# Linear attention with elu+1 features: v loaded straight into a padded tile, relu(k) on GpSimd

## The chip, the cores and the metric

The kernel runs on one core of one Trainium2 chip. The metric is the device time of one execution in microseconds, taken as a median over runs. The engines are TensorE (PE), VectorE (DVE), ScalarE (ACT), GpSimd (POOL) and SyncE (SP); SyncE here only issues DMAs, which 16 DMA engines carry out.

## What is computed

There are 32 heads (B = 1, H = 32) of S = 2048 tokens with D = 128, all in bfloat16. Each of q, k, v and the output has 16.8 MB.

```python
phi_q = jnp.where(q > 0, q + 1, jnp.exp(q)) + 1e-6
phi_k = jnp.where(k > 0, k + 1, jnp.exp(k)) + 1e-6
kv  = jnp.einsum("bhsd,bhse->bhde", phi_k, v)
z   = jnp.einsum("bhsd->bhd", phi_k)
num = jnp.einsum("bhqd,bhde->bhqe", phi_q, kv)
den = jnp.einsum("bhqd,bhd->bhq", phi_q, z)[..., None] + 1e-6
return num / den
```

The attention is not causal: each head sums a 128x128 matrix kv over all tokens and then applies it to every query.

## The kernel before

**Layout.** A head's 2048 tokens lie on 128 partitions with 16 tokens each, so a head of q, k or v is a tile of 128 x 16 x 128 elements, 4 KB a partition. Tokens are permuted over partitions by this in the same way everywhere, and the sums don't mind.

**The feature map in two parts.** phi(x) is computed as (min(exp(x), 1) + 1e-6) + relu(x). ScalarE makes exp (`ek`, line 350; `eq`, line 386), VectorE the min and the add in place (`em`, line 353; `emq`, line 388). relu(k) is made into the tile `rk_sb`: the first 8 of the 16 tokens by VectorE (`rkd`, line 356), the last 8 by GpSimd (`rkp`, line 360). relu(q) comes from PSUM after the transpose, half by ScalarE (`rqa`, line 392) and half by VectorE (`rqb`, line 395). The two parts are never added: PE multiplies each and accumulates.

**v and its ones.** To get z with the same products, v has a column of ones beside its 128 columns. v is loaded into `v_sb`, packed; GpSimd copies it to `v1_sb` (`v1`, line 364), where a token has 136 elements (128 of v, then ones, written once at the start by `v1ones`, line 315, two memsets for the two buffers). `v1_sb` has two buffers, `v_sb` seven.

**PE** does for each head: 16 transposes of q (`T`, line 382), 32 products of 129 columns for kv and z (`kv`, line 371, two halves `kv.0` and `kv.1`: 16 tokens times the two parts), and 38 products for the output (`n`, lines 403, 408, 410, in two groups). ScalarE brings kv from PSUM to SBUF (`kvs`, line 376). VectorE takes the reciprocal of the denominators (`r`, line 417) and multiplies into the output tile (`f`, line 424), in two groups, of 12 and of 4 tokens. SyncE stores a head (`st`, line 432).

**Order.** Each engine has a list of operations, written out by hand in `ORDER`, which it executes in that order. An operation waits on semaphores for what it depends on: data, and buffers (`freed`) that must have been used up. q, k and v have 7 buffers each (`NI`), the output 12 (`NO`), exp(k) and relu(k) 2. On GpSimd there is one more rule, `gate`: from the fourth head on, the copy of v of head h waits for `r(h-3).0` and relu(k) of head h for `f(h-3).0`, which sets them beside certain VectorE instructions.

**DMAs.** SyncE issues all loads but the first of v (ScalarE) and all stores, in one list, in which the stores lie some way behind the loads: `st12` follows `ldv24`, and after the last load (`ldq31`) the stores of heads 19 to 31 are left. A load reads 32 runs of 16 KB (four partitions each) and writes 128 rows of 4 KB, each to one partition:

```python
runs = bass.AP(t.tensor, t.offset, [[RUN * NT * D, P // RUN], [1, RUN * NT * D]])
flat = bass.AP(to.tensor, to.offset, [list(to.ap[0]), [1, NT * D]])
```

Of the kernel before, what the change touches and what calls it, by code (L numbers as in the profile page):

```python
# [6 lines left out]
P = 128  # L7
# [1 line left out]
ENGINES = ("PE", "DVE", "ACT", "POOL", "SP")  # L9
NH = 32  # L10
BY_ACT = ('ldv0.0',)
NI, NO, NE, NR, NV, NQ, NK = 7, 12, 2, 2, 2, 2, 2
WARM = (15, 4, 4)
RUN = 4
QUEUE = {mybir.EngineType.SP: "qSPDynamicHW", mybir.EngineType.Activation: "qActDynamicHW"}
HALVES = ((0, 8), (8, 16))
# [3 lines left out]
def k_parts(h):  # L20
    return HALVES if h == 0 else WHOLE
# [3 lines left out]
    return WHOLE  # L25


v_parts = k_parts


def q_parts(h):
    return HALVES if h == 0 else ((0, 8), (8, 12), (12, 16)) if h == NH - 1 else WHOLE
# [3 lines left out]
    return HALVES  # L36


RKP = (8, 8, 8, 8, 8, 8, 8, 8, 8, 8, 8, 8, 8, 8, 8, 8, 8, 8, 8, 8, 8, 8, 8, 8, 8, 8, 8, 8, 8, 8, 8, 8)
NA = (8, 8, 8, 8, 8, 8, 8, 8, 8, 8, 8, 8, 8, 8, 8, 8, 8, 8, 8, 8, 8, 8, 8, 8, 8, 8, 8, 8, 8, 8, 8, 16)  # L40


def rkp_parts(h):
    return ((16 - RKP[h], 16),) if RKP[h] else ()


def rkd_parts(h):
    return tuple((a, min(b, 16 - RKP[h])) for a, b in k_parts(h) if a < 16 - RKP[h])

# [12 lines left out]
    return ((0, 6), (6, 12), (12, 16)) if h == NH - 1 else WHOLE  # L62


def gate(name, h):
    if h < 3:
        return []
    return [f"r{h - 3}.0"] if name == "v1" else [f"f{h - 3}.0"]


BANK = ((0, 8), (8, 16))
# [6 lines left out]
def rqb_parts(h):  # L78
    if na(h) == 16:
        return ()  # L80
    if h == NH - 1:
# [15 lines left out]
        n30.0 n30.1 n31.0 n31.1 n31.2  # L97
    """,
    "DVE": """
        ones eps0 rkd0.0 em0.1 em0.0 eps1 v1ones0 eps2 rkd1.0 rqb0.0 emq0.1 v1ones1 em1.0 emq0.0 rkd2.0 rqb1.0 em2.0  # L100
        emq1.0 rkd3.0 r0.0 f0.0 em3.0 rqb2.0 r0.1 rkd4.0 f0.1 r1.0 emq2.0 f1.0 em4.0 rqb3.0 r1.1 rkd5.0 f1.1 r2.0
        emq3.0 f2.0 em5.0 rqb4.0 r2.1 rkd6.0 f2.1 r3.0 emq4.0 f3.0 em6.0 rqb5.0 r3.1 rkd7.0 f3.1 r4.0 emq5.0 f4.0
        em7.0 rqb6.0 r4.1 rkd8.0 f4.1 r5.0 emq6.0 f5.0 em8.0 rqb7.0 r5.1 rkd9.0 f5.1 r6.0 emq7.0 f6.0 em9.0 rqb8.0
        r6.1 emq8.0 f6.1 r7.0 rkd10.0 f7.0 em10.0 rqb9.0 r7.1 rkd11.0 f7.1 r8.0 emq9.0 f8.0 em11.0 rqb10.0 r8.1
        rkd12.0 f8.1 r9.0 emq10.0 f9.0 em12.0 rqb11.0 r9.1 rkd13.0 f9.1 r10.0 emq11.0 f10.0 em13.0 rqb12.0 r10.1
        rkd14.0 f10.1 r11.0 emq12.0 f11.0 em14.0 rqb13.0 r11.1 rkd15.0 f11.1 r12.0 emq13.0 f12.0 em15.0 rqb14.0
        r12.1 rkd16.0 f12.1 r13.0 emq14.0 f13.0 em16.0 rqb15.0 r13.1 rkd17.0 f13.1 r14.0 emq15.0 f14.0 em17.0
        rqb16.0 r14.1 rkd18.0 f14.1 r15.0 emq16.0 f15.0 em18.0 rqb17.0 r15.1 rkd19.0 f15.1 r16.0 emq17.0 f16.0
        em19.0 rqb18.0 r16.1 f16.1 rkd20.0 r17.0 emq18.0 f17.0 em20.0 rqb19.0 r17.1 f17.1 emq19.0 r18.0 rkd21.0
        f18.0 em21.0 r18.1 rqb20.0 f18.1 rkd22.0 r19.0 emq20.0 f19.0 em22.0 r19.1 rqb21.0 f19.1 emq21.0 r20.0  # L110
        rkd23.0 f20.0 em23.0 r20.1 rqb22.0 f20.1 emq22.0 r21.0 rkd24.0 f21.0 em24.0 rqb23.0 r21.1 f21.1 emq23.0
        r22.0 rkd25.0 f22.0 em25.0 rqb24.0 r22.1 rkd26.0 f22.1 r23.0 emq24.0 f23.0 em26.0 r23.1 rqb25.0 f23.1
        emq25.0 r24.0 rkd27.0 f24.0 em27.0 r24.1 rqb26.0 f24.1 rkd28.0 r25.0 emq26.0 f25.0 em28.0 r25.1 rqb27.0
        f25.1 emq27.0 r26.0 rkd29.0 f26.0 em29.0 rqb28.0 r26.1 rkd30.0 f26.1 r27.0 emq28.0 f27.0 em30.0 r27.1
        rqb29.0 f27.1 rkd31.0 r28.0 emq29.0 f28.0 em31.0 rqb30.0 r28.1 f28.1 r29.0 emq30.0 f29.0 emq31.0 r29.1 f29.1
        emq31.1 r30.0 f30.0 r30.1 f30.1 emq31.2 r31.0 f31.0 r31.1 f31.1 r31.2 f31.2
    """,
    "ACT": """
        exp ldv0.0 ek0.1 ek0.0 eq0.1 rqa0 eq0.0 ek1.0 eq1.0 kvs0 ek2.0 rqa1 kvs1 ek3.0 eq2.0 kvs2 rqa2 ek4.0 eq3.0 kvs3 rqa3
# [6 lines left out]
        ek30.0 eq29.0 kvs29 rqa29 ek31.0 eq30.0 kvs30 rqa30 eq31.0 eq31.1 kvs31 eq31.2 rqa31  # L126
    """,
    "POOL": """
        ident0 ident rkp1.0 rkp0.0 v10.0 v10.1 v11.0 v12.0 rkp2.0 v13.0 rkp3.0 v14.0 rkp4.0 v15.0 rkp5.0 v16.0
        rkp6.0 v17.0 rkp7.0 v18.0 rkp8.0 v19.0 rkp9.0 v110.0 rkp10.0 v111.0 rkp11.0 v112.0 rkp12.0 v113.0 rkp13.0  # L130
        v114.0 rkp14.0 v115.0 rkp15.0 v116.0 rkp16.0 v117.0 rkp17.0 v118.0 rkp18.0 v119.0 rkp19.0 v120.0 rkp20.0
        v121.0 rkp21.0 v122.0 rkp22.0 v123.0 rkp23.0 v124.0 rkp24.0 v125.0 rkp25.0 v126.0 rkp26.0 v127.0 rkp27.0
        v128.0 rkp28.0 v129.0 rkp29.0 v130.0 rkp30.0 v131.0 rkp31.0
    """,
    "SP": """
        ldk0.0 ldq0.0 ldk1.0 ldq1.0 ldv1.0 ldk2.0 ldv2.0 ldq2.0 ldk3.0 ldv3.0 ldk4.0 ldq3.0 ldv4.0 ldk5.0
# [22 lines left out]
class Program:  # L159
# [10 lines left out]
    def add(self, eng, key, fn, deps=(), dma=None, inc=True):  # L170
        assert key not in self.op, key
        self.op[key] = (eng, fn, tuple(deps), dma, inc)
# [71 lines left out]
def bass_standalone__linear_attn_elu__prompt_kernel(nc: bass.Bass, q: bass.AP, k: bass.AP, v: bass.AP, out: bass.AP):  # L244
    B, H, S, D = q.shape
    assert D == P and S == 16 * P and B * H == NH
    NT = S // P
    bf16, fp32, i32 = mybir.dt.bfloat16, mybir.dt.float32, mybir.dt.int32
    NC = D + 1
    NW = D + 8  # L250
    BIG = 3.4028234663852886e38

    qf, kf, vf, of = (t.rearrange("b h s d -> (b h) s d") for t in (q, k, v, out))
    rows = lambda t, h: t[h].rearrange("(p j) d -> p j d", j=NT)

    with ExitStack() as es:
# [8 lines left out]
            return es.enter_context(nc.semaphore(f"la_s{names[0]}"))  # L265

        sb = lambda shape, dt=bf16: alloc(nc.sbuf_tensor, shape, dt)
        k_sb, q_sb, v_sb = (sb([P, NI, NT, D]) for _ in range(3))
        em_sb, rk_sb = sb([P, NE, NT, D]), sb([P, NR, NT, D])
        v1_sb = sb([P, NV, NT, NW])  # L270
        emq_sb, rq_sb = sb([P, NQ, NT, D]), sb([P, NQ, NT, D])
        kvs_sb = sb([P, NK, NW])
        rden_sb = sb([P, 2, NT], fp32)
        o_sb = sb([P, NO, NT, D])
        ident, ones, epsr = sb([P, P]), sb([P, P]), sb([P, 3])
# [4 lines left out]
        kv_ps = o_ps[:, KV0:KV0 + NC]  # L280

        pr = Program(sem)
        add = pr.add

        def over(name, h, parts, t0, t1):
            return [f"{name}{h}.{i}" for i, (a, b) in enumerate(parts(h)) if a < t1 and t0 < b]

        def every(name, h, parts):
            return [f"{name}{h}.{i}" for i in range(len(parts(h)))]

        def freed(n, h, *names):
            return [d for name, parts in names for d in every(name, h - n, parts)] if h >= n else []

        def fs(h, banks):
            return [f"f{h}.{i}" for i, (t0, nb, n, b0) in enumerate(groups(h))
                    if set(banks) & set(range(b0, b0 + nb))]
# [4 lines left out]
        def rks(h, t0=0, t1=NT):  # L301
            return over("rkd", h, rkd_parts, t0, t1) + over("rkp", h, rkp_parts, t0, t1)
# [8 lines left out]
        add("DVE", "eps2", lambda g: g.memset(epsr[32:33, :], ec), ["eps0"])  # L311
        add("DVE", "ones", lambda g: g.memset(ones[:], 1.0))
        add("ACT", "exp", lambda e: e.activation(first_sb[:, 0:1], ones[:, 0:1], ACT.Exp), ["ones"])
        for s in range(NV):
            add("DVE", f"v1ones{s}", lambda g, s=s: g.memset(v1_sb[:, s, :, D:D + 2], 1.0))

        def warm(key, n):
            def g(e):
# [13 lines left out]

        def load(name, dst, src, h, i, t0, t1, last):
            t = src[h]
            runs = bass.AP(t.tensor, t.offset, [[RUN * NT * D, P // RUN], [1, RUN * NT * D]])
            to = dst[:, h % NI]
            flat = bass.AP(to.tensor, to.offset, [list(to.ap[0]), [1, NT * D]])
            add("ACT" if f"ld{name}{h}.{i}" in BY_ACT else "SP", f"ld{name}{h}.{i}", lambda e: copy(e, flat, runs),
                last, dma=f"{name}{h % NI}.{i}")

        def head(h):
# [2 lines left out]
            for i, (a, b) in enumerate(ld_parts(h)):  # L344
                load("q", q_sb, qf, h, i, a, b, freed(NI, h, ("T", t_parts)))
            for i, (a, b) in enumerate(ld_parts(h)):
                load("v", v_sb, vf, h, i, a, b, freed(NI, h, ("v1", v_parts)))

            for i, (a, b) in enumerate(k_parts(h)):
                add("ACT", f"ek{h}.{i}", lambda e, a=a, b=b: e.activation(  # L350
# [8 lines left out]
            for i, (a, b) in enumerate(rkp_parts(h)):  # L359
                add("POOL", f"rkp{h}.{i}", lambda e, a=a, b=b: e.tensor_scalar(  # L360
                    rk_sb[:, h % NR, a:b], k_sb[:, h % NI, a:b], BIG, 0.0, op0=ALU.min, op1=ALU.max),
                    over("ldk", h, ld_parts, a, b) + freed(NR, h, ("kv", kv_parts)) + gate("rkp", h))
            for i, (a, b) in enumerate(v_parts(h)):
                add("POOL", f"v1{h}.{i}", lambda e, a=a, b=b: e.tensor_copy(  # L364
                    v1_sb[:, h % NV, a:b, 0:D].bitcast(i32), v_sb[:, h % NI, a:b].bitcast(i32)),
                    over("ldv", h, ld_parts, a, b) + freed(NV, h, ("kv", kv_parts)) + gate("v1", h))
            for i, (a, b) in enumerate(kv_parts(h)):
                def g(e, a=a, b=b):
                    for j in range(a, b):
                        for part, src in ((0, em_sb[:, h % NE]), (1, rk_sb[:, h % NR])):  # L370
                            ins = e.matmul(kv_ps, lhsT=src[:, j], rhs=v1_sb[:, h % NV, j, 0:NC],  # L371
                                           start=(j + part == 0), stop=(j == NT - 1 and part == 1))
                    return ins
                add("PE", f"kv{h}.{i}", g, over("em", h, k_parts, a, b) + rks(h, a, b) + over("v1", h, v_parts, a, b)
                    + [f"v1ones{h % NV}"] + ([f"kvs{h - 1}"] if h else []) + (fs(h - 3, [5]) if h >= 3 else []))
            add("ACT", f"kvs{h}", lambda e: e.activation(kvs_sb[:, h % NK, 0:NC], kv_ps, ACT.Copy),  # L376
                every("kv", h, kv_parts) + freed(NK, h, ("n", groups)))

# [99 lines left out]
```

## Time and profile before

| | |
|---|---|
| median of 3 runs | 171.18 us (170.42 to 171.69) |
| the profiled execution | 169.46 us, its span 168.2 us |
| granted TensorE clock | 0.996 |
| busy: PE, DVE, ACT, POOL | 158.9, 152.0, 153.6, 86.2 us |
| DMA | 67.53 MB in 9532 packets, mean 402 GB/s; the queue of the loads and stores has 96.6% of 16 engines |
| HBM | 50.33 MB read, 16.78 MB written |
| GpSimd: relu(k), copies of v | 32 x 1387 ns, 33 x 1253 ns |
| VectorE: relu(k) | 32 x 435 ns |
| issue to landing, median | k 18.8, q 19.7, v 19.2, stores 19.1 us |

How to read it: the times come from one execution under the profiler. The span runs from the first to the last instruction; the execution's time has some 1.3 us more around it. "Busy" is time in which an engine executes something. A group line gives line, engine, operation, tiles, shapes and count, then the busy time, the mean of one in ns, the engine's idle time before, and what ended that. A line of waits gives who waited for whom, the total in us, how often, and the longest. A line of a timeline gives start, duration, engine, line, operation and count. In the lines of slices each digit is the busy share of one fortieth of the span in tenths. Counts of packets go by reads: a load's 16 KB run is one packet, whatever rows it is written to.

### The profile page before, as it was taken

To read this page: it belongs to the slowest core of one execution; us is meant where nothing else is said; L and a number is where in the kernel's file an instruction comes from. 1 tells how busy PE (TensorE), PEld (TensorE's weight loads), DVE (VectorE), ACT (ScalarE), POOL (GpSimd) and SP (SyncE) were. 2 spreads that over 40 slices of the span, in tenths; PEclk is the share of its full clock that TensorE was granted. 3 is DMA by queue.
4 is the path that set the end of the run, shared out by engine and by line. 5 is a ranking of instruction groups with operands and counts; after the bars stand their busy time and mean duration, and the time that the engine had idled before them with its cause. 6 is when DMAs were issued, how large, how long until landed. Compare 5 with 4: busy or idle time off the path is not lost.

```text
span 168.2 us, 6309 instructions
## 1 busy us (share of the span) xinstructions
PE 158.9 (94%) x2775; PEld 153.4 (91%) x2775; DVE 152.0 (90%) x267; ACT 153.6 (91%) x134; POOL 86.2 (51%) x71
## 2 busy tenths in 40 slices
PE   6599999999999999999999999999999999999960
PEld 2358999999999999999999999999999999999950
DVE  0444989999999999999999999999999999999895
ACT  3698999999999999999999999999999999999630
POOL 1094365566554655566555664565545564556000
PEclk9999999999999999999999999999999999999998
DMA  5999999999999999999999999999999999999977
GB/s 207 417 425 401 417 401 405 413 409 405 415 413 405 399 427 416 399 424 435 399 425 414 414 422 422 415 417 421 410 431 422 391 427 416 409 416 412 382 292 271
DMA packets 9532, 67.53 MB, mean 402 GB/s; under 512 B 2080, under 2 KB 2464, under 8 KB 6432
## 3 DMA queue, kind: packets, MB, share of 16 engines
q1 hardware_dynamic: 9456, 66.59, 96.6%
q8 instruction: 22, 0.36, 0.9%
q10 hardware_dynamic: 48, 0.52, 0.7%
q14 instruction: 6, 0.05, 0.1%
HBM read 50.33 MB, written 16.78 MB: 399 GB/s over the span
## 4 chain that ended last, share of the span: by engine, by line
PE 91%; DVE 4%; DMA 3%; issue 0%; SPq 0%
PE la L371 35%; PE la L408 19%; PE la L382 18%; PE la L410 17%; DMA la<-in_q_dram 3%; DVE la L424 3%; PE la L320 2%; PE la L403 1%; DVE la L417 0%; SPq L329 0%; DVE la L388 0%
## 5 line engine op out<-in xcount | busy, mean ns | idle before, releaser
L424 DVE TENSOR_TENSOR la<-la 128x1536 bf16<-128x1536 f32 (+2 forms) x65 | 77.6, 1194 | 0.4
L410 PE MATMUL la<-la 128*128 128x129 bf16 x512 | 67.7, 219 | 0.0
L408 PE MATMUL la<-la 128*128 128x129 bf16 x512 | 67.7, 218 | 0.0
L386 ACT ACTIVATE la<-la 128x2048 bf16<-128x2048 bf16 (+2 forms) x35 | 60.5, 1731 | 4.4 <-PE la L382 2.7
L371 PE MATMUL la<-la 128*128 128x129 bf16 x1024 | 63.3, 220 | 0.5 <-issue 0.4
L350 ACT ACTIVATE la<-la 128x2048 bf16<-128x2048 bf16 (+1 forms) x33 | 61.3, 1860 | 2.0 <-DMA la<-in_k_dram 2.0
L360 POOL TENSOR_SCALAR la<-la 128x1024 bf16<-128x1024 bf16 x32 | 44.3, 1387 | 31.3 <-DVE la L424 24.7
L364 POOL COPY la<-la 128x1024 int32<-128x1024 int32 (+1 forms) x33 | 41.2, 1253 | 36.9 <-DVE la L417 34.5
L371 PEld LDWEIGHTS la<-la 128*128 128x128 bf16 x1024 | 59.3, 98 | 0.8 <-issue 0.8
L410 PEld LDWEIGHTS la<-la 128*128 128x128 bf16 x512 | 49.3, 96 | 0.0
L408 PEld LDWEIGHTS la<-la 128*128 128x128 bf16 x512 | 47.0, 97 | 0.0
L382 PE MATMUL la<-la 128*128 128x128 bf16 x512 | 34.6, 222 | 1.8 <-DMA la<-in_q_dram 1.8
L403 PE MATMUL la<-la 128*128 128x3 bf16 (+1 forms) x192 | 32.3, 168 | 1.6 <-DVE la L424 1.6
L392 ACT ACTIVATE la<-la 128x1024 bf16<-128x1024 bf16 (+1 forms) x32 | 33.4, 1045 | 0.0
L382 PEld LDWEIGHTS la<-la 128*128 128x128 bf16 x512 | 29.9, 99 | 3.3 <-DMA la<-in_q_dram 2.7
L353 DVE TENSOR_SCALAR la<-la 128x2048 bf16<-128x2048 bf16 (+1 forms) x33 | 22.0, 666 | 4.1 <-ACT la L350 4.1
L395 DVE TENSOR_SCALAR la<-la 128x1024 bf16<-128x1024 bf16 x31 | 21.1, 681 | 1.9 <-ACT la L386 1.4
L388 DVE TENSOR_SCALAR la<-la 128x2048 bf16<-128x2048 bf16 (+2 forms) x35 | 21.7, 619 | 0.0
L403 PEld LDWEIGHTS la<-la 128*128 128x128 bf16 x192 | 18.7, 98 | 1.8 <-DVE la L424 1.8
L356 DVE TENSOR_SCALAR la<-la 128x1024 bf16<-128x1024 bf16 x32 | 13.9, 435 | 5.8 <-DMA la<-in_k_dram 4.3
L417 DVE RECIPROCAL la<-la 128x12 f32<-128x12 f32 (+2 forms) x65 | 12.8, 196 | 1.2 <-ACT la L376 0.6
L376 ACT ACTIVATE la<-la 128x129 bf16<-128x129 f32 x32 | 9.1, 283 | 0.5 <-PE la L371 0.5
(15 smaller groups left out, 12.9 us busy)
## 6 DMA issues: line engine op xcount, KB each, us to landing
la<-in_k_dram SPq DMA_DIRECT2D x32, 512.0 KB, 18.8
la<-in_q_dram SPq DMA_DIRECT2D x32, 512.0 KB, 19.7
la<-in_v_dram SPq DMA_DIRECT2D x31, 512.0 KB, 19.2
out_dram<-la SPq DMA_DIRECT2D x31, 512.0 KB, 19.1
la<-in_v_dram ACTq DMA_DIRECT2D x1, 512.0 KB, 4.4
out_dram<-la SPq DMA_DIRECT2D x2, 192.0 KB, 2.6
out_dram<-la SPq DMA_DIRECT2D x1, 128.0 KB, 1.9
```

The source lines that it names most:

```text
L350: add("ACT", f"ek{h}.{i}", lambda e, a=a, b=b: e.activation(em_sb[:, h % NE, a:b], k_sb[:, h % NI, a:b], ACT.Exp), over("ldk", h, ld_parts ...
L353: add("DVE", f"em{h}.{i}", lambda e, a=a, b=b: e.tensor_scalar(em_sb[:, h % NE, a:b], em_sb[:, h % NE, a:b], 1.0, EPS, op0=ALU.min, op1=AL ...
L360: add("POOL", f"rkp{h}.{i}", lambda e, a=a, b=b: e.tensor_scalar(rk_sb[:, h % NR, a:b], k_sb[:, h % NI, a:b], BIG, 0.0, op0=ALU.min, op1=A ...
L364: add("POOL", f"v1{h}.{i}", lambda e, a=a, b=b: e.tensor_copy(v1_sb[:, h % NV, a:b, 0:D].bitcast(i32), v_sb[:, h % NI, a:b].bitcast(i32)), ...
L371: ins = e.matmul(kv_ps, lhsT=src[:, j], rhs=v1_sb[:, h % NV, j, 0:NC], start=(j + part == 0), stop=(j == NT - 1 and part == 1))
L382: ins = e.transpose(xT[:, j], q_sb[:, h % NI, j], ident[:])
L386: add("ACT", f"eq{h}.{i}", lambda e, a=a, b=b: e.activation(emq_sb[:, h % NQ, a:b], xT[:, a:b], ACT.Exp), over("T", h, t_parts, a, b) + fr ...
L392: add("ACT", f"rqa{h}", lambda e: e.activation(rq_sb[:, h % NQ, 0:n], xT[:, 0:n], ACT.Relu), over("T", h, t_parts, 0, n) + freed(NQ, h, (" ...
L403: e.matmul(_ap(o_ps[:, :], o + D, [[NC, m]]), lhsT=ones[:], rhs=epsr[:, 0:m], start=True, stop=False, skip_group_check=True)
L408: e.matmul(to, lhsT=emq_sb[:, h % NQ, t], rhs=kvs_sb[:, h % NK, 0:NC], start=False, stop=False, skip_group_check=True)
L410: ins = e.matmul(to, lhsT=rq_sb[:, h % NQ, t], rhs=kvs_sb[:, h % NK, 0:NC], start=False, stop=True, skip_group_check=True)
L424: return e.tensor_tensor(out=_ap(o_sb[:, :, :, :], first(o_sb[:, h % NO, t0, 0:1]) - first(o_sb[:, :, :, :]), [[m * D, nb], [D, m], [1, D] ...
```

## The change

- `v_sb` and the copy `v1` are gone. `v1_sb` has 7 buffers, and a token in it has 256 elements (`VP`), 512 bytes: v in the first 256 bytes, the ones after it.
- A load of v still reads 32 runs of 16 KB, but writes 16 pieces of 256 bytes to each partition, 2048 in all.
- `kv` waits for the load itself. A load of v waits for `kv` of seven heads before, where it waited for the copy of seven heads before.
- The ones are written by two memsets over 1 and 6 buffers, where it was one buffer each.
- From the fourth head on GpSimd does both halves of relu(k), as two instructions: the first with the copy's gate (`r(h-3).0`), the second with the old one (`f(h-3).0`). VectorE's `rkd` of these heads is gone. In all lists the rest keeps its order.

```diff
-NI, NO, NE, NR, NV, NQ, NK = 7, 12, 2, 2, 2, 2, 2
+NI, NO, NE, NR, NQ, NK = 7, 12, 2, 2, 2, 2
-RKP = (8, 8, 8, 8, ...
+RKP = (8,) * 3 + (16,) * 29
 def rkp_parts(h):
-    return ((16 - RKP[h], 16),) if RKP[h] else ()
+    return HALVES[2 - RKP[h] // 8:]
-def gate(name, h):
-    if h < 3:
-        return []
-    return [f"r{h - 3}.0"] if name == "v1" else [f"f{h - 3}.0"]
+def gate(h, i):
+    return [f"{'rf'[i]}{h - 3}.0"] if h >= 3 else []
 "DVE"
-        emq1.0 rkd3.0 r0.0 f0.0 em3.0 rqb2.0 r0.1 rkd4.0 f0.1 r1.0 emq2.0 f1.0 em4.0 ...
+        em2.0 emq1.0 r0.0 f0.0 em3.0 rqb2.0 r0.1 f0.1 r1.0 emq2.0 f1.0 em4.0 ...
 "POOL"
-        ident0 ident rkp1.0 rkp0.0 v10.0 v10.1 v11.0 v12.0 rkp2.0 v13.0 rkp3.0 v14.0 rkp4.0 ...
+        ident0 ident rkp1.0 rkp0.0 rkp2.0 rkp3.0 rkp3.1 rkp4.0 rkp4.1 rkp5.0 rkp5.1 ...
+    VP = 256
-        k_sb, q_sb, v_sb = (sb([P, NI, NT, D]) for _ in range(3))
+        k_sb, q_sb = (sb([P, NI, NT, D]) for _ in range(2))
-        v1_sb = sb([P, NV, NT, NW])
+        v1_sb = sb([P, NI, NT, VP])
-        for s in range(NV):
-            add("DVE", f"v1ones{s}", lambda g, s=s: g.memset(v1_sb[:, s, :, D:D + 2], 1.0))
+        for s, (a, b) in enumerate(((0, 1), (1, NI))):
+            add("DVE", f"v1ones{s}", lambda g, a=a, b=b: g.memset(v1_sb[:, a:b, :, D:D + 2], 1.0))
-            runs = bass.AP(t.tensor, t.offset, [[RUN * NT * D, P // RUN], [1, RUN * NT * D]])
+            runs = bass.AP(t.tensor, t.offset, [[RUN * NT * D, P // RUN]] + [[1, 1]] * (name == "v") + [[1, RUN * NT * D]])
-            flat = bass.AP(to.tensor, to.offset, [list(to.ap[0]), [1, NT * D]])
+            flat = bass.AP(to.tensor, to.offset, [list(to.ap[0])] + ([[VP, NT], [1, D]] if name == "v" else [[1, NT * D]]))
-                load("v", v_sb, vf, h, i, a, b, freed(NI, h, ("v1", v_parts)))
+                load("v", v1_sb, vf, h, i, a, b, freed(NI, h, ("kv", kv_parts)))
-                    over("ldk", h, ld_parts, a, b) + freed(NR, h, ("kv", kv_parts)) + gate("rkp", h))
-            for i, (a, b) in enumerate(v_parts(h)):
-                add("POOL", f"v1{h}.{i}", lambda e, a=a, b=b: e.tensor_copy(...
+                    over("ldk", h, ld_parts, a, b) + freed(NR, h, ("kv", kv_parts)) + gate(h, i))
-                            ins = e.matmul(kv_ps, lhsT=src[:, j], rhs=v1_sb[:, h % NV, j, 0:NC],
+                            ins = e.matmul(kv_ps, lhsT=src[:, j], rhs=v1_sb[:, h % NI, j, 0:NC],
-                add("PE", f"kv{h}.{i}", g, over("em", h, k_parts, a, b) + rks(h, a, b) + over("v1", h, v_parts, a, b)
-                    + [f"v1ones{h % NV}"] + ...
+                add("PE", f"kv{h}.{i}", g, over("em", h, k_parts, a, b) + rks(h, a, b) + over("ldv", h, ld_parts, a, b)
+                    + [f"v1ones{int(h > 0)}"] + ...
```

More of the change, by code (lines that the diff above doesn't have):

```diff
@@ L25, in ld_parts @@
     return WHOLE
-v_parts = k_parts
 def q_parts(h):
@@ L36, in kv_parts @@
     return HALVES
-RKP = (8, 8, 8, 8, 8, 8, 8, 8, 8, 8, 8, 8, 8, 8, 8, 8, 8, 8, 8, 8, 8, 8, 8, 8, 8, 8, 8, 8, 8, 8, 8, 8)
+RKP = (8,) * 3 + (16,) * 29
 NA = (8, 8, 8, 8, 8, 8, 8, 8, 8, 8, 8, 8, 8, 8, 8, 8, 8, 8, 8, 8, 8, 8, 8, 8, 8, 8, 8, 8, 8, 8, 8, 16)
 def rkp_parts(h):
-    return ((16 - RKP[h], 16),) if RKP[h] else ()
+    return HALVES[2 - RKP[h] // 8:]
 def rkd_parts(h):
@@ L99 @@
     "DVE": """
[L100 to L114, printed above, removed]
@@ L115 @@
-        rqb29.0 f27.1 rkd31.0 r28.0 emq29.0 f28.0 em31.0 rqb30.0 r28.1 f28.1 r29.0 emq30.0 f29.0 emq31.0 r29.1 f29.1
-        emq31.1 r30.0 f30.0 r30.1 f30.1 emq31.2 r31.0 f31.0 r31.1 f31.1 r31.2 f31.2
+        ones eps0 rkd0.0 em0.1 em0.0 eps1 v1ones0 eps2 rkd1.0 rqb0.0 emq0.1 v1ones1 em1.0 emq0.0 rkd2.0 rqb1.0
+        em2.0 emq1.0 r0.0 f0.0 em3.0 rqb2.0 r0.1 f0.1 r1.0 emq2.0 f1.0 em4.0 rqb3.0 r1.1 f1.1 r2.0 emq3.0 f2.0
+        em5.0 rqb4.0 r2.1 f2.1 r3.0 emq4.0 f3.0 em6.0 rqb5.0 r3.1 f3.1 r4.0 emq5.0 f4.0 em7.0 rqb6.0 r4.1 f4.1
@@ new lines @@
+        r5.0 emq6.0 f5.0 em8.0 rqb7.0 r5.1 f5.1 r6.0 emq7.0 f6.0 em9.0 rqb8.0 r6.1 emq8.0 f6.1 r7.0 f7.0 em10.0
+        rqb9.0 r7.1 f7.1 r8.0 emq9.0 f8.0 em11.0 rqb10.0 r8.1 f8.1 r9.0 emq10.0 f9.0 em12.0 rqb11.0 r9.1 f9.1
+        r10.0 emq11.0 f10.0 em13.0 rqb12.0 r10.1 f10.1 r11.0 emq12.0 f11.0 em14.0 rqb13.0 r11.1 f11.1 r12.0
+        emq13.0 f12.0 em15.0 rqb14.0 r12.1 f12.1 r13.0 emq14.0 f13.0 em16.0 rqb15.0 r13.1 f13.1 r14.0 emq15.0
+        f14.0 em17.0 rqb16.0 r14.1 f14.1 r15.0 emq16.0 f15.0 em18.0 rqb17.0 r15.1 f15.1 r16.0 emq17.0 f16.0
@@ new lines @@
+        em19.0 rqb18.0 r16.1 f16.1 r17.0 emq18.0 f17.0 em20.0 rqb19.0 r17.1 f17.1 emq19.0 r18.0 f18.0 em21.0
+        r18.1 rqb20.0 f18.1 r19.0 emq20.0 f19.0 em22.0 r19.1 rqb21.0 f19.1 emq21.0 r20.0 f20.0 em23.0 r20.1
+        rqb22.0 f20.1 emq22.0 r21.0 f21.0 em24.0 rqb23.0 r21.1 f21.1 emq23.0 r22.0 f22.0 em25.0 rqb24.0 r22.1
+        f22.1 r23.0 emq24.0 f23.0 em26.0 r23.1 rqb25.0 f23.1 emq25.0 r24.0 f24.0 em27.0 r24.1 rqb26.0 f24.1
+        r25.0 emq26.0 f25.0 em28.0 r25.1 rqb27.0 f25.1 emq27.0 r26.0 f26.0 em29.0 rqb28.0 r26.1 f26.1 r27.0
@@ L117 @@
+        emq28.0 f27.0 em30.0 r27.1 rqb29.0 f27.1 r28.0 emq29.0 f28.0 em31.0 rqb30.0 r28.1 f28.1 r29.0 emq30.0
+        f29.0 emq31.0 r29.1 f29.1 emq31.1 r30.0 f30.0 r30.1 f30.1 emq31.2 r31.0 f31.0 r31.1 f31.1 r31.2 f31.2
     """,
@@ L128 @@
     "POOL": """
[L129 to L133, printed above, removed]
+        ident0 ident rkp1.0 rkp0.0 rkp2.0 rkp3.0 rkp3.1 rkp4.0 rkp4.1 rkp5.0 rkp5.1 rkp6.0 rkp6.1 rkp7.0 rkp7.1
+        rkp8.0 rkp8.1 rkp9.0 rkp9.1 rkp10.0 rkp10.1 rkp11.0 rkp11.1 rkp12.0 rkp12.1 rkp13.0 rkp13.1 rkp14.0
+        rkp14.1 rkp15.0 rkp15.1 rkp16.0 rkp16.1 rkp17.0 rkp17.1 rkp18.0 rkp18.1 rkp19.0 rkp19.1 rkp20.0 rkp20.1
+        rkp21.0 rkp21.1 rkp22.0 rkp22.1 rkp23.0 rkp23.1 rkp24.0 rkp24.1 rkp25.0 rkp25.1 rkp26.0 rkp26.1 rkp27.0
+        rkp27.1 rkp28.0 rkp28.1 rkp29.0 rkp29.1 rkp30.0 rkp30.1 rkp31.0 rkp31.1
     """,
@@ L361, in head @@
                     rk_sb[:, h % NR, a:b], k_sb[:, h % NI, a:b], BIG, 0.0, op0=ALU.min, op1=ALU.max),
-                    over("ldk", h, ld_parts, a, b) + freed(NR, h, ("kv", kv_parts)) + gate("rkp", h))
-            for i, (a, b) in enumerate(v_parts(h)):
-                add("POOL", f"v1{h}.{i}", lambda e, a=a, b=b: e.tensor_copy(
-                    v1_sb[:, h % NV, a:b, 0:D].bitcast(i32), v_sb[:, h % NI, a:b].bitcast(i32)),
-                    over("ldv", h, ld_parts, a, b) + freed(NV, h, ("kv", kv_parts)) + gate("v1", h))
+                    over("ldk", h, ld_parts, a, b) + freed(NR, h, ("kv", kv_parts)) + gate(h, i))
             for i, (a, b) in enumerate(kv_parts(h)):
@@ L370, in g @@
                         for part, src in ((0, em_sb[:, h % NE]), (1, rk_sb[:, h % NR])):
-                            ins = e.matmul(kv_ps, lhsT=src[:, j], rhs=v1_sb[:, h % NV, j, 0:NC],
+                            ins = e.matmul(kv_ps, lhsT=src[:, j], rhs=v1_sb[:, h % NI, j, 0:NC],
                                            start=(j + part == 0), stop=(j == NT - 1 and part == 1))
                     return ins
-                add("PE", f"kv{h}.{i}", g, over("em", h, k_parts, a, b) + rks(h, a, b) + over("v1", h, v_parts, a, b)
-                    + [f"v1ones{h % NV}"] + ([f"kvs{h - 1}"] if h else []) + (fs(h - 3, [5]) if h >= 3 else []))
+                add("PE", f"kv{h}.{i}", g, over("em", h, k_parts, a, b) + rks(h, a, b) + over("ldv", h, ld_parts, a, b)
+                    + [f"v1ones{int(h > 0)}"] + ([f"kvs{h - 1}"] if h else []) + (fs(h - 3, [5]) if h >= 3 else []))
             add("ACT", f"kvs{h}", lambda e: e.activation(kvs_sb[:, h % NK, 0:NC], kv_ps, ACT.Copy),
```

## The prediction

> **What bounds the kernel now.** I read the page from the top: the busy shares, the slices, the DMA queues. Four engines are near 90%, so shares alone rule nothing out; but two lines of the slices stand out: the 16 DMA engines are full from the second slice to the tail, and PE from the third.
>
> ```profile
> span 168.2 us, 6309 instructions
> ...
> PE 158.9 (94%) x2775; PEld 153.4 (91%) x2775; DVE 152.0 (90%) x267; ACT 153.6 (91%) x134; POOL 86.2 (51%) x71
> ...
> PE   6599999999999999999999999999999999999960
> ...
> DMA  5999999999999999999999999999999999999977
> ...
> q1 hardware_dynamic: 9456, 66.59, 96.6%
> ...
> PE 91%; DVE 4%; DMA 3%; issue 0%; SPq 0%
> ```
>
> The chain that ended last (last line) runs through PE. So next I asked for busy time by stage, to see whether PE has any gap that a faster neighbour could close, and whether the DMA engines have any slack beside it.
>
> ```profile
> core 0: us, PE busy (x) PEld busy (x) DVE busy (x) ACT busy (x) POOL busy (x), PEclk, DMA share, GB/s
> ...
> 152.00:158.00 6.00, 6.00 (x113) 5.99 (x111) 5.97 (x10) 4.31 (x6) 2.31 (x2) 1.00 1.03 417
> 60.00:150.00 90.00, 90.00 (x1651) 89.72 (x1649) 89.33 (x155) 90.00 (x79) 51.84 (x39) 1.00 1.01 417
> ```
>
> From 60 to 150 us PE is busy 90.00 of 90.00 us at full clock, at 4.70 us a head (the chain's transposes start 4.70 us apart). The DMA share in the same row is 1.01: the DMA engines have no pause either, and move 417 GB/s. A transfer of 512 KB (0.524 MB) takes 0.524 / 0.417 = 1.26 us of them. The third view is SyncE's timeline at the end, with the time to landing of the last load:
>
> ```profile
> 129.96 3.80 SPq L329 DMA_DIRECT2D la<-in_q_dram  x1
> 133.81 32.77 SPq L432 DMA_DIRECT2D out_dram<-la  x15
> ...
> DMA to landing us min/median/max: 21.6/21.6/21.6
> ```
>
> The last load (q of head 31) is issued at 129.96 and lands 21.6 us later, at 151.5, because some 16 transfers stand in the queue ahead of it. Behind it come the last 13 heads' stores, 13 x 0.524 = 6.8 MB, which at 417 GB/s need 16.3 us: 151.5 + 16.3 = 167.8, against the span's end at 168.2. So the DMA queue ends where the compute chain ends. There are two limits at one height, and whatever is added to the queue's work is added to the time; what is taken from PE's neighbours is not taken from it.
>
> **The change part by part.**
>
> *GpSimd's copies (line 364) go:* 31 x 1.288 + 2 x 0.706 = 41 us of GpSimd. *Relu halves move to GpSimd:* 29 more of line 360 at 1.387 = 40.2 us. Per head GpSimd has 1.39 + 1.39 = 2.77 us instead of 1.29 + 1.39 = 2.68, inside a head of 4.70 us. The first half takes the slot and the gate (r of head h-3) that the copy had, the second half keeps its own (f.0 of head h-3):
>
> ```profile
> POOL la L364 <- DVE la L417: 34.5, 29, 1.8
> POOL la L360 <- DVE la L424: 24.7, 29, 0.9
> ```
>
> GpSimd stood 59 us at these two gates; nothing queues behind them but its own next head. For head 12 the copy starts at 62.04 and the relu at 64.27 (to 65.7), and kv12 starts on PE at 67.3, its second half at 68.2. The first relu has 3.8 us of cover, the second 2.5. Cost 0; without the cover every us over is paid 29 times.
>
> *VectorE loses 29 relu halves (line 356):* 29 x 0.435 = 12.6 us. VectorE was 99% busy from 60 to 150 us, but PE has no gap there that ends on it, so this gives 0 while PE and the queue set the pace; with that cover gone, the other way round, it would be worth up to 12.6 us. The ones are written in 112 rows instead of 32: the second memset grows from 32 elements (85 ns) to 192, at most 6 x 85 = 0.5 us, and stands before VectorE's 1.85 us wait for ScalarE at 10.6 us. Cost 0.
>
> *Waits.* kv waits for v's landing itself and not for a copy of it. v of head 31 lands at 149.1, its copy started at 151.5 and kv31 at 156.6: a step less, not on the path. A v load on SyncE now waits until kv of seven heads before has ended, not until its copy has. SyncE's queue is in order, so all loads and stores behind wait too. Setting issues against PE's rows, the worst case is v of head 15: issued at 46.6, while kv8 ends at 50.4, some 3.9 us late. The queue in front holds 17 to 20 us of transfers by then, so the DMA engines see no pause. Cost 0; with a queue shorter than 4 us these waits would come through.
>
> *The v transfer itself.* It still reads 16 KB runs, 32 of them, two for each of 16 DMA engines; but where each run was written as 4 rows of 4 KB, it is now written as 64 pieces of 256 bytes: 60 more writes for each packet, 60 x 64 = 3840 more for each DMA engine over 32 heads. Nothing in this trace writes such pieces, so I bound the price of one. The trace's packet records give: 4 KB stores 159 ns (median), the last head's 1.5 KB and 1 KB stores 65 and 45 ns, the 4-byte semaphore writes 9 ns. From 1 KB to 4 KB that is 114 ns for 3072 bytes, 0.0371 ns a byte, and 45 - 38 = 7 ns for a packet, its read and its write together. A 16 KB packet with one write should then take 7 + 608 = 615 ns. With its four writes the median is 625, the fastest cluster 611, and where only loads run 640.
> - Lower end: 611 ns says three more writes cost nothing; and were all v packets to run at 611 in place of 625, 64 x 14 ns = 0.9 us would even be won. No row has a faster one.
> - Upper end: (640 - 615) / 3 = 8.3 ns a write, near the 7 ns of a whole packet. 3840 x 8.3 = 31.9 us.
> - Taken: the median, (625 - 615) / 3 = 3.3 ns a write: 60 x 3.3 = 200 ns more for a packet of 625, 0.40 us for a load of 1.26, and 32 x 0.40 = **12.8 us** in all. I take it because it comes from packets of the very kind that is changed, in the mix of loads and stores that fills most of the span.
>
> The Trainium skill speaks against this change. Its page "DMA: Bandwidth & Descriptors", section "Specifications", puts line rate at 512 bytes and more, below which an engine reads before it writes; were that to double v's transfer time, the estimate is 64 x 608 ns = 39 us more. The same page, "Why small descriptors are slow (HBM only)", is milder: some 3 cycles of bus for each packet, 11 for a 256-byte one instead of 8, which makes 3/8 of 608 ns, 14.6 us in all by estimate, and it says that SBUF-to-SBUF transfers don't suffer. No row of this trace shows either at 256 bytes.
>
> **Sum.** The profiled execution took 169.46 us (span 168.2 and 1.3 around it). 0 (GpSimd) + 0 (VectorE) + 0 (waits) + 12.8 (queue) = 182.3 us. The median of the runs shown, 171.18, lies 1.7 above that execution, so against the median I say 171.2 + 12.8 = **184.0 us**. The queue takes the added time whole, since it has no slack at the end. PE will fall behind the loads: they land 2.5 to 4 us before their use in the second half, and by head 31 they come 12 us later, so PE waits some 9 us in all, beside the queue and not on top of it.
>
> **The rivals.**
> - *The writes hide under the read stream* (not slower). Place: the DMA engine's write side, which has 9.5 ns of bytes for each 256-byte piece to do its bookkeeping in. For it: the 611 ns cluster with four writes. Against it: medians of 625 and 640. Price 0, so the queue ends as before: 171.2 us, or 170.3 with the lower end. It decides while a write costs under 1.7 us / 3840 = 0.44 ns; faster by more than 1% it hardly gets, since the queue still has 66.6 MB to move and PE its 4.70 us a head.
> - *Each write pays like a packet of its own.* For it: 1 KB packets, at 22.8 GB/s an engine against 26.2 for 16 KB, show that small pieces do cost. Against it: four writes per 16 KB cost less than this in the mixed stretches. 3840 x 7 ns = 26.9 us: 198 us, and 203 at 8.3 ns.
> - *The change doesn't do what it says:* the read side is cut to 256 bytes as well. A 256-byte packet would take 7 + 9.5 = 16.5 ns, 64 of them 1056 instead of 625: 431 ns x 64 = 27.6 us, 199 us. The packet count of the queue would tell it: 2048 for a v load instead of 32.
> - *GpSimd becomes the bound:* it would need a relu half of 1.4 + 2.5 = 3.9 us before kv waits for it, and then 29 us for each further us. The same instruction takes 1.42 us in that slot now; against it stands all of the trace.
>
> **How the numbers follow.** This kernel's measurement can tell about 1%, 1.7 us, from no change. Writes at 1 to 5 ns (3.8 to 19.2 us, 175 to 190 us): 0.50. Hidden, or under 1 ns: 0.17, of which 0.13 lies within 1% and 0.03 below it. Like packets: 0.25. Cut reads: 0.05. GpSimd: 0.03. The likeliest case's own range is 175 to 190; to hold the time 8 times in 10 the range reaches to both bounds of the unknown price, 170.3 and 203. Faster 0.03, same 0.13, slower 0.84.
>
> **What would show it.** Right: queue q1 keeps its packet count (some 9456) and a share near 97% of a span near 181 us; from 60 to 150 us DMA share stays about 1 while the rate falls from 417 to about 4 x 0.524 / (4 x 1.26 + 0.40) = 385 GB/s; PE shows idle in front of line 382's transposes or the kv products, ended by DMA; GpSimd has some 85 us, VectorE some 139. Wrong: PE still 90 of 90 us and 417 GB/s (hidden), a rate below 360 GB/s in the middle (writes like packets), a queue with tens of thousands of packets more (cut reads), or kv waiting for GpSimd.

## The result, and the profile after

The changed kernel takes 224.38 us (median of 4 runs, 223.41 to 226.68) against 171.01 us: 1.314 times the time, 95% interval 1.302 to 1.326, 53.4 us more. An execution can fall into a slower state at a lower granted clock (in one kernel below 187.6 us at 0.976, against 184.5 at 0.991); where two runs differ so, the faster one counts. The forecast was 184.0 with an upper end of 203. The direction was right, the size far too small. The page of the profiled execution (226.68 us), the lines that answer to those of before:

```profile
span 225.3 us, 6300 instructions
...
PE 174.8 (78%) x2775; PEld 166.4 (74%) x2775; DVE 146.5 (65%) x238; ACT 156.1 (69%) x134; POOL 79.5 (35%) x67
...
PE   5599999199997974999395994399958777859950
...
DMA  6999899899987998998899877989799999999996
...
q1 hardware_dynamic: 9456, 66.59, 90.3%
...
PE 39%; DMA 27%; SPq 16%; ACT 10%; DVE 5%; issue 2%; DVEq 0%
```

The queue moves the same bytes in the same 9456 packets, so the reads were not cut. Its packets' time is 90.3% of 225.3 = 203.4 us for each engine, where it was 96.6% of 168.2 = 162.5: the packets got 41 us longer. The span grew by 57, so about 16 us more are pauses in which the DMA engines have nothing. The middle, by stage (busy time of PE, PEld, DVE, ACT and POOL, then granted clock, DMA share, GB/s):

```profile
60.00:150.00 90.00, 69.61 (x1129) 68.32 (x1127) 58.74 (x93) 63.08 (x53) 36.06 (x27) 0.89 0.90 292
```

A rate of 292 GB/s where it was 417, and a DMA share of 0.90 where it was 1.01: both the longer packets and the pauses show in one line. PE has fallen from 90.00 to 69.61 us busy. Who waits for whom:

```profile
PE la L373 <- DMA la<-in_q_dram: 34.4, 12, 6.8
```

The transposes wait for q, whose own transfer wasn't changed at all. SyncE's timeline shows where the time goes (start, duration):

```profile
120.66 0.59 SPq L423 DMA_DIRECT2D out_dram<-la  x1
121.29 0.56 SPq L324 DMA_DIRECT2D la<-in_v_dram  x1
121.95 7.94 SPq L324 DMA_DIRECT2D la<-in_k_dram  x1
129.94 0.89 SPq L324 DMA_DIRECT2D la<-in_v_dram  x1
130.87 3.24 SPq L423 DMA_DIRECT2D out_dram<-la  x1
```

The issue of a v load itself takes 0.56 and 0.89 us. The instruction after it is held for 7.94 us, the one after the next v for 3.24. Over the 25 v loads from 20 us on that a transfer of another kind follows, this following issue takes 4.42 us on average, before the change 0.99. What holds it is not a buffer: the one of the k load that was held for 7.94 us had been free since 87.3 us, when GpSimd ended relu(k) of seven heads before. From 20 to 200 us every load and store is issued after its buffer or its output was ready, and SyncE's issues fill 176 of the 180 us; before the change it stood idle for buffers, for those of k alone seven times and 20 us in all. And the queue in front of the engines has shrunk (loads from 20 to 200 us, the first of the kernel before):

```profile
DMA to landing us min/median/max: 15.2/19.7/21.6
```

And the same of the changed one:

```profile
DMA to landing us min/median/max: 4.7/7.1/11.3
```

The median has gone from 19.7 to 7.1 us.

### The profile page after: what moved, and what is told of

Read it like the earlier page. It is cut to its first block, busy times and chain, and to the rows that moved or that the text cites. A ratio compares the mean times of both kernels' runs of the same rounds, so it can differ in the third digit from the quotient of the medians.

```text
span 225.3 us, 6300 instructions
## 1 busy us (share of the span) xinstructions
PE 174.8 (78%) x2775; PEld 166.4 (74%) x2775; DVE 146.5 (65%) x238; ACT 156.1 (69%) x134; POOL 79.5 (35%) x67
## 3 DMA queue, kind: packets, MB, share of 16 engines
q1 hardware_dynamic: 9456, 66.59, 90.3%
## 4 chain that ended last, share of the span: by engine, by line
PE 39%; DMA 27%; SPq 16%; ACT 10%; DVE 5%; issue 2%; DVEq 0%
DMA la<-in_q_dram 23%; PE la L362 14%; SPq L324 12%; PE la L373 10%; PE la L399 7%; PE la L401 6%; ACT la L377 5%; SPq L423 4%; DMA la<-in_k_dram 3%; ACT la L345 3%; DVE la L415 3%; PE la L315 2%; ACT la L383 1%; DVE la L386 1%; DVE la L379 1%
## 5 line engine op out<-in xcount | busy, mean ns | idle before, releaser
L355 POOL TENSOR_SCALAR la<-la 128x1024 bf16<-128x1024 bf16 x61 | 78.8, 1294 | 125.4 <-DVE la L408 75.8
L362 PE MATMUL la<-la 128*128 128x129 bf16 x1024 | 71.2, 234 | 0.4 <-issue 0.4
L399 PE MATMUL la<-la 128*128 128x129 bf16 x512 | 69.8, 221 | 0.8 <-issue 0.8
L401 PE MATMUL la<-la 128*128 128x129 bf16 x512 | 70.1, 223 | 0.0
L373 PE MATMUL la<-la 128*128 128x128 bf16 x512 | 37.4, 231 | 39.5 <-DMA la<-in_q_dram 34.4
L362 PEld LDWEIGHTS la<-la 128*128 128x128 bf16 x1024 | 67.5, 106 | 0.6 <-issue 0.6
L373 PEld LDWEIGHTS la<-la 128*128 128x128 bf16 x512 | 32.3, 104 | 43.1 <-issue 11.4
L401 PEld LDWEIGHTS la<-la 128*128 128x128 bf16 x512 | 50.0, 98 | 0.0
L399 PEld LDWEIGHTS la<-la 128*128 128x128 bf16 x512 | 48.0, 99 | 0.9 <-issue 0.9
L386 DVE TENSOR_SCALAR la<-la 128x1024 bf16<-128x1024 bf16 x31 | 21.2, 684 | 32.5 <-ACT la L377 32.5
L348 DVE TENSOR_SCALAR la<-la 128x2048 bf16<-128x2048 bf16 (+1 forms) x33 | 22.5, 681 | 11.8 <-ACT la L345 11.8
L394 PEld LDWEIGHTS la<-la 128*128 128x128 bf16 x192 | 19.3, 100 | 1.8 <-DVE la L415 1.8
L315 PE MATMUL la<-la 128*128 128x480 bf16 x23 | 8.3, 538 | 1.5 <-POOL la L300 1.5
L315 PEld LDWEIGHTS la<-la 128*128 128x128 bf16 x23 | 3.0, 136 | 5.6 <-issue 3.7
```

The source lines that it names most:

```text
L362: ins = e.matmul(kv_ps, lhsT=src[:, j], rhs=v1_sb[:, h % NI, j, 0:NC], start=(j + part == 0), stop=(j == NT - 1 and part == 1))
L373: ins = e.transpose(xT[:, j], q_sb[:, h % NI, j], ident[:])
L394: e.matmul(_ap(o_ps[:, :], o + D, [[NC, m]]), lhsT=ones[:], rhs=epsr[:, 0:m], start=True, stop=False, skip_group_check=True)
L399: e.matmul(to, lhsT=emq_sb[:, h % NQ, t], rhs=kvs_sb[:, h % NK, 0:NC], start=False, stop=False, skip_group_check=True)
L401: ins = e.matmul(to, lhsT=rq_sb[:, h % NQ, t], rhs=kvs_sb[:, h % NK, 0:NC], start=False, stop=True, skip_group_check=True)
```

## The experiments

**The loads alone.** A kernel without any computing: SyncE issues groups of eight loads with different pieces, as described.

```diff
+for b in range(8): copy(dst(b, [[256, 16], [1, 128]]), src(v, b, [[8192, 32], [1, 1], [1, 8192]]))   # group B
+wait()
+for b in range(8): copy(dst(b, [[512, 8], [1, 256]]), src(q, b, ...))                                # group C
+...
```

> Nothing is computed; SyncE issues loads of 512 KB in groups of eight, with a wait after each group, and then 32 stores of zeros. The groups: A reads of 16 KB, writes of 4 KB; B as v in the changed kernel (256-byte writes at a pitch of 512); C, E, F pieces of 512 bytes, 1 KB and 2 KB at twice their size; G reads of 256 bytes too; H reads of 4 KB; I as B, each load cut into two of 64 partitions; J as B on 8 of the 16 DMA engines; K two times three plain loads and one as B; L stores. Theory 1 (each 256-byte write costs an engine about 20 ns, twice its bytes; the 633 ns by which v's packets are longer, over 60 writes): A 8 x 1.27 = 10 us and some 2 of latency; B 8 x 2.5 = 20 and 2; I the same; C back to 10 to 12 if 20 ns is a floor for one write, 15 if it is 10 ns on top of the bytes; E and F 10 to 12; J 40, since each engine has twice the writes. Theory 2 (the queue holds only some 128 writes for each engine, so one v load fills it, SyncE can't issue ahead and the engines drain between transfers; the write itself costs little): B 20 or more, but I, whose loads fill half a queue each, clearly less, 12 to 15; C 12; the issues show it: in A some 16 loads could stand in the queue, in C two, in E four. Theory 3 (the writes' descriptors are made at about 1.1 ns each for all engines together): B 20, J 20 too.

The middle of the groups A, B, C, E, G and J, by stage (the last two columns are DMA share and GB/s):

```profile
4.00:14.00 10.00, 0.00 (x0) 0.00 (x0) 1.00 0.93 344
18.00:35.00 17.00, 0.00 (x0) 0.00 (x0) 1.00 1.00 216
39.00:52.00 13.00, 0.00 (x0) 0.00 (x0) 1.00 0.98 282
56.00:67.00 11.00, 0.00 (x0) 0.00 (x0) 1.00 0.98 334
86.00:102.00 16.00, 0.00 (x0) 0.00 (x0) 1.00 1.32 218
154.00:187.00 33.00, 0.00 (x0) 0.00 (x0) 1.00 0.49 113
```

The 256-byte pieces (second row) move at 216 GB/s, about half of the 417 of the kernel before (the 344 of the first row is no steady rate: its packets took 708 ns on average and 625 in the median, the longer ones at the start). The packet records give the median 16 KB packet by pieces: 4 KB 625 ns, 2 KB 675, 1 KB 751, 512 bytes 901, 256 bytes 1207. From 625 to 1207 are 60 more writes, 9.7 ns each; from 625 to 901 are 28, 9.9 each. So there is neither a floor nor a threshold between 256 bytes and 4 KB: each write adds some 10 ns to its bytes. Reads of 256 bytes (fifth row) make no difference, 218 GB/s; the share of 1.32 there means that the records of these small packets overlap. Groups F and H, 2 KB pieces and reads of 4 KB, ran at 355 and 219 GB/s. On 8 of 16 engines (last row) the rate halves to 113, so each engine pays for its own writes and theory 3 falls. Cutting each load in two (group I) did not help: 192 GB/s, so for loads on their own theory 2 falls too. Theory 1 stands, as a price on top of the bytes. The issues show the short queue as well: in A no issue took over 0.9 us, in B the second took 1.55 us and the later ones 2.2 to 2.4, in C the fourth was the first over 1 us, in E the seventh. Group K has three plain loads, one v load, three plain ones and a v load again:

```profile
189.54 1.80 SPq L23 DMA_DIRECT2D m_buf<-in_k_dram  x3
191.38 0.60 SPq L23 DMA_DIRECT2D m_buf<-in_v_dram  x1
192.02 6.20 SPq L23 DMA_DIRECT2D m_buf<-in_k_dram  x3
```

Ahead of the v load three issues take 1.80 us, behind it 6.20, of which 4.92 are the first. Nothing is computed here, so one v load is enough to hold what follows it.

**More pieces alone.** The same frame with other pitches and smaller pieces.

```diff
+copy(dst(b, [[128, 16], [1, 128]]), ...)   # N: 256 B packed       +copy(dst(b, [[136, 16], [1, 128]]), ...)  # O: pitch 272
+copy(dst(b, [[128, 32], [1, 64]]), ...)    # Q: 128 B at 256       +R: as the change, SyncE and ScalarE by turns
```

> Nothing is computed; groups of eight loads of 512 KB, all with reads of 16 KB: M 256-byte writes at a pitch of 512 as in the changed kernel, N the same packed at 256, O at 272, Q 128-byte writes at 256, R as M by turns from SyncE and ScalarE; then 32 stores of zeros. With 9.7 ns for each write on top of the bytes (586 ns a packet): M 1207 ns a packet, N the same if it is the number of writes that costs and not the pitch, Q 586 + 128 x 9.7 = 1830. O is as M, or dearer if a piece that starts off a 256-byte line costs more. R as M in all, 2.35 us a load, if the engines set the pace; less if the single queue does.

Groups M, N and Q by stage:

```profile
4.00:21.00 17.00, 0.00 (x0) 0.00 (x0) 1.00 1.00 216
26.00:42.00 16.00, 0.00 (x0) 0.00 (x0) 1.00 1.02 219
70.00:85.00 15.00, 0.00 (x0) 0.00 (x0) 1.00 0.84 209
```

Packed pieces of 256 bytes, without a gap, are as slow as those at 512 (219 and 216), and a pitch of 272 is no worse (222). It is the number of writes that costs, and the pitch nothing. Q missed my expectation: pieces of 128 bytes run at 209 GB/s, 9.8 ns for each, 4.7 of them bytes. With a DMA share of 0.84 some of this is pauses; the median packet took 1049 ns, 8.2 for each write. The price of 10 ns on top does not go on below 256 bytes. R, two queues and nothing but v loads, is no faster (213 GB/s).

> Nothing is computed; groups of eight loads with reads of 16 KB: S 128-byte writes at 256 (again), T 64-byte writes at 128, U 4 KB as in the kernel; then 32 stores. With half the rate for any piece of 256 bytes or less (128 took about as long in all as 256): S and T both near 2.4 us a load. With a price for each write below 128 bytes: T up to 4.5.

The 128-byte group came out the same again (210 GB/s), but 64-byte pieces (`dst(b, [[64, 64], [1, 32]])`) at 116 GB/s, 8.8 ns each: half the rate did not hold there. At 128 and 64 bytes the time is some 8 to 10 ns for a write, whatever its size. Why the price is 9.7 on top of the bytes at 256 and above, and 8 to 10 in all at 128 and below, I did not find out.

**The parts of the change.** First v's load with VectorE's half of relu(k) as before:

```diff
-RKP = (8,) * 3 + (16,) * 29
+RKP = (8,) * 32            # and the DVE and POOL lists with rkd and one rkp for each head, gate f
```

> The changed kernel, but VectorE does its half of relu(k) for all heads as before, and GpSimd only the other half. If v's transfer is the whole loss: 224 us, within 2. If the moved relu had a share in it (kv waits for GpSimd), less, by that share.

229.7 us, ratio 1.353 (1.345 to 1.360): 5 us slower than the whole change, which neither expectation had. VectorE now stands at relu(k) for a late k, with the finishing of the output behind it in its list:

```profile
DVE la L349 <- DMA la<-in_k_dram: 17.6, 6, 5.6
```

VectorE has no relu(k) there in the changed kernel from the fourth head on. But this wait is not shown to be the cause, and the trace speaks against it: the last load is issued at 206.7 us, in the changed kernel at 202.8, so most of the loss is in the loads already, and here too SyncE waits for no buffer from 20 to 200 us. Why the loads go out more slowly stays open. Then the rest of the change without v's load:

```diff
-load("v", v1_sb, ...)      # 256-byte writes
+load("v", v_sb, ...)       # packed, 4 KB writes
-rhs=v1_sb[:, h % NI, j, 0:NC]
+rhs=v1_sb[:, h % 2, j, 0:NC]    # a constant tile
...
```

> The changed kernel, but v is loaded packed, in 4 KB writes as before, into its own tile, and kv multiplies a constant tile of ones in place of v (it still waits for v's landing); the copy is gone as in the changed kernel. If v's transfer is the whole loss, the rest of the change is worth nothing: 171 us, within 1. If the relu move or the lost copies matter, up to 2% to either side.

169.97 us, ratio 1.0014 (0.9984 to 1.0044): nothing. From 60 to 150 us PE is as full as before and the DMA engines too, while VectorE has 5 us less:

```profile
60.00:150.00 90.00, 89.85 (x1646) 89.41 (x1644) 84.24 (x134) 89.81 (x78) 51.09 (x39) 1.00 1.01 417
```

So the whole loss is v's load, and relief of VectorE and GpSimd is worth nothing while PE and the DMA engines are both full.

**The size of the pieces, in the kernel.** v1 with one column of ones for two tokens (512 bytes), and for four (1 KB):

```diff
-v1_sb = sb([P, NI, NT, VP])
+v1_sb = sb([P, NI, NT // 2, 2 * VP])      # NT // 4, 4 * VP
...
```

> The changed kernel, but v comes in pieces of 512 bytes (two tokens) at a pitch of 1 KB, the ones behind the second; the even tokens' ones column is wrong. Theory 1 with a floor of some 20 ns a write: 512 bytes take 19 ns anyway, so 171 to 175 us. Theory 1 with 10 ns on top of each write: 28 more writes a packet, 64 x 280 ns = 18 us, 189. Theory 2 (the queue): two such loads fill it instead of one, so part of the loss stays, 185 to 200 us, with issue to landing between the 7 us of the changed kernel and the 19 of the one before.

Two runs took 184.5 and 187.6 us, before 170.0 on the same chip: by the first +14.5 us, near the 18 of a price on top of each write's bytes, far from the 0 to 4 of a floor, and just under the least that the queue theory gave (15). The trace is of the second:

```profile
60.00:150.00 90.00, 82.75 (x1470) 81.69 (x1468) 76.17 (x121) 81.06 (x69) 44.20 (x35) 0.98 1.01 374
```

The DMA share is 1.01 again. The queue is shorter than before the change, as the queue theory wanted it (9 to 11 us from issue to landing), but in this stretch it does not run empty, so the price of the writes explains the loss without pauses.

> As the run with 512-byte pieces, with pieces of 1 KB (four tokens) at 2 KB, the ones behind the fourth; three of four ones columns are wrong. By the price found in the loads alone, 751 ns for such a packet against 625, 64 packets an engine: 170 + 64 x 0.126 = 178 us, and no pauses, since four such loads fill the queue. If the price in the kernel were not the one found alone, or the pauses went on, over 182.

174.56 us, ratio 1.029 (1.026 to 1.032): +4.8 us where 8 were expected. In the kernel a write costs 4.8 us / (64 x 12) = 6.3 ns at 1 KB and 14.5 / (64 x 28) = 8.1 at 512 bytes, a little less than the 10 found in loads alone.

**Where the pauses come from.** The list of all 130 transfers in its order, without computing, v in pieces or packed:

```diff
+PACKED = False     # True
+for key in LIST: load(...) or e.dma_start(...)    # a load waits only for the one before it in its buffer
```

> Nothing is computed: the changed kernel's list of transfers alone, in its order and with v in 256-byte pieces, a load waiting only for the load before it in the same buffer, stores of zeros. The 53 us split into some 37 us of longer v packets (60 more writes at 9.7 ns, 64 packets an engine) and some 16 us in which the DMA engines stand (share 0.90 from 60 to 150 us). Theory P1 (a v load's 128 writes an engine fill the queue, SyncE is held, the following transfer starts late: the pauses come from the queue alone): 215 to 225 us, the instruction after each v load held for some 4 us, as in the changed kernel. Theory P2 (the pauses come with the waits between the short queue and the computing engines): 163 + 37 = 200 us and a DMA share near 1.

> The same list alone with v packed, in 4 KB writes as before: 33.5 MB read and written at the pace of the kernel before, 163 to 168 us. What the two lists differ by is the whole price of the 256-byte writes without any computing: 37 us by P2, 50 or more by P1.

Packed 167.5 us, in pieces 215.3, one run each: 47.8 of the 53.4 us are there without any computing. From 60 to 150 us, first packed:

```profile
60.00:150.00 90.00, 0.00 (x0) 0.00 (x0) 1.00 1.01 417
```

and in pieces:

```profile
60.00:150.00 90.00, 0.00 (x0) 0.00 (x0) 1.00 0.97 312
```

Packed, the engines run without a pause at the very rate of the kernel; in pieces the share is 0.97, and the issue after a v load takes 4.28 us against 1.09. By the time, P1 is right. By the pauses it is only in part: the share fell to 0.97 here and to 0.90 in the kernel. By the two pages (share of q1 and q10 times the span) the packets take 206.7 us of each engine where they took 164.5 when packed, 42 us more, and only some 6 of the 48 are pauses. Then v in a queue of its own, first the list alone:

```diff
-load(e, "v", h)             # nc.sync, in the list
+load(nc.scalar, "v", h)     # all v loads from ScalarE, as buffers allow
```

> The list of transfers alone, v in 256-byte pieces, but all v loads are issued by ScalarE, as fast as their seven buffers allow, and SyncE issues the rest. The list alone took 215.3 us with v in the one queue and 167.5 with v packed. If the pauses behind v loads go and the price of the writes stays: 167.5 + 37 = 205. If a second queue also fills the engines' time between two small writes: clearly less, 175 to 195. If the writes fill something that both queues share: 215.

199.3 us (one run), here from 20 to 100 us:

```profile
20.00:100.00 80.00, 0.00 (x0) 0.00 (x0) 1.00 1.01 325
```

The pauses are gone and the writes' price stays, a little lower: 31.8 us over the packed list, 31.8 / 3840 = 8.3 ns a write. And in the kernel:

```diff
-BY_ACT = ('ldv0.0',)
+BY_ACT = ('ldv0.0',) + tuple(f'ldv{h}.0' for h in range(7, 32))    # in ACT's list after kvs(h-7)
...
```

> The changed kernel, but the loads of v from head 7 on are issued by ScalarE (after kvs of seven heads before), so that their writes stand in another queue than k, q and the stores. P1: SyncE is not held any more behind a v load, the pauses go and the writes' price stays: 171 + 37 = 208 us, a DMA share near 1, issue to landing of k and q well over the 7 us of the changed kernel. If the writes fill something that both queues share, or the pauses have another cause: 220 us or more.

206.2 us, ratio 1.213 (1.197 to 1.229), where 208 were expected:

```profile
60.00:150.00 90.00, 82.49 (x1449) 79.78 (x1447) 73.25 (x118) 80.45 (x68) 42.95 (x32) 0.99 1.01 347
```

The share is 1.01 again and the rate 347 in place of 292. From issue to landing a load takes 23.3 us again (median from 60 to 190 us). Taking v's pieces out of the queue of k, q and the stores gives 18 us back, with every small write still there.

## Why the prediction was wrong

**The sum of the 53.4 us, by the runs:** 31.8 us for the writes themselves (v in pieces in a queue of its own against the packed list, 199.3 - 167.5); 16.0 us because they stand in one queue with the other transfers (215.3 - 199.3); the remaining 5.6 us come only with the computing, and how is not shown: SyncE waits for no buffer from 20 to 200 us, so late engines do not hold its loads back. The 16.0 us of the queue are not the 16 us of pauses of the changed kernel, though the numbers agree. By the pages the packets take 164.5 us of each engine in the packed list, 197.3 with two queues and 206.7 in one, so more than half of the 16.0 are again longer packets, and most of the kernel's pauses appear only with the computing. Why a packet takes longer in the one queue stays open. In the list with two queues the v loads also run further ahead, so the border between the first two terms is not exact; the kernel with two queues puts them at 36 and 18.

**The step that failed: "The queue in front holds 17 to 20 us of transfers by then, so the DMA engines see no pause. Cost 0; with a queue shorter than 4 us these waits would come through."** I took the queue of 17 to 20 us as cover, and did not ask whether the change takes that cover away. It does: a v load now has 128 writes for each engine where it had 8, SyncE is held behind it for 4.4 us on average, and the queue falls to some 7 us from issue to landing. The waits that this step weighed, of a v load for kv of seven heads before, did not come through: from 20 to 200 us there is none. What came is the holding of SyncE by the queue itself, at 7 us and not under 4. The working named the cover, and left out that the same edit multiplies by 16 what the queue has to hold. That is the reason why the time lies outside the range: no end of it had a term for the queue.

**The term that was mis-sized: a write at 3.3 ns.** It is 8.3 ns by the list with two queues, 6.3 to 8.1 in the kernel with larger pieces, 9.7 for v loads alone. The bounds were 0, 3.3 and 8.3, and the upper one came near, but in part by luck: it rests on 640 ns where only loads run, but the packed list has a median of 640 with loads and stores mixed, and group A, plain loads alone, one of 625, which by the same working gives 3.3 again. I chose the median of the mixed stretches because it was of "the very kind that is changed"; but a difference of 10 ns for three extra writes lay under a spread of 611 to 640 ns, and 60 writes multiply what three can't resolve.

**What held.** Two limits at one height: the packed list alone takes 167.5 of the kernel's 170 us. GpSimd and VectorE at 0: 1.0014 with v packed. With v in pieces the same move was worth 5 us (224.4 against 229.7), within the "up to 12.6 us" that the working gave it where the cover is gone. "The queue takes the added time whole": yes. PE falls behind the loads and waits for q: yes, but 34.4 us of it where some 9 were expected. The rival "each write pays like a packet of its own" (198 to 203) came nearest, and its price was right in size; "reads cut" is refuted by 9456 packets, and would have cost nothing more, since reads of 256 bytes ran at 218 GB/s against 216. GpSimd as the bound and hidden writes are out.

**The rule that spoke against it.** In the Trainium skill, the line rate from 512 bytes on ("DMA: Bandwidth & Descriptors", "Specifications") gave 39 us by estimate, and at 256 bytes the rate is indeed about half, 216 GB/s. But 512-byte pieces ran at 282 and 1 KB pieces at 334, so the measurement shows a price for each write and no step at 512. The 3 cycles for each packet ("Why small descriptors are slow (HBM only)", on the same page) gave 14.6 us by estimate, less than half of the 31.8.

## What to carry to other kernels

Count a transfer by its writes as well as by its bytes: here each write of 256 bytes to 1 KB added some 6 to 11 ns to an engine, so 256-byte pieces ran at about half the rate, at pitches of 256, 272 and 512 bytes and with reads of 256 bytes, 4 KB and 16 KB. When a step is costed at nothing because something covers it (here a queue 19 us deep), ask whether the same change shrinks the cover; a v load of 16 times as many writes held the issuing engine and delayed transfers that were not touched. And relief for engines beside two full ones was worth nothing here, at a ratio of 1.0014.

## What I had not expected of the hardware

- The cost is the writes' alone: reads of 16 KB and of 256 bytes ran at the same 216 and 218 GB/s when the writes were of 256 bytes.
- Pieces of 128 bytes were about as fast as those of 256 (209 and 216 GB/s), those of 64 half as fast (116).
- The queue's depth is not one number. Some 16 loads of 4 KB rows stood in it before the change; after, even the stores at the end, with no v load left, landed 7.8 us after their issue (median from 206 to 216 us), and stores on their own 5.3 us. What sets it beyond the count of writes stays open.
- The granted clock of TensorE fell to 0.89 from 60 to 150 us, where PE was busy 77% of the time, and to 0.81 in a stretch of the run with v in ScalarE's queue where it was busy 64%; it is 1.00 where PE is full.
